# Loading part of q in two transfers: 120 tokens and 8 tokens

## The chip, the cores and the metric

The kernel runs on one core of a Trainium2 chip. A core has five engines that run side by side and wait for each other by semaphores: TensorE (PE, matmuls; its weight loads are shown as PEld), VectorE (DVE), ScalarE (ACT), GpSimd (POOL) and SyncE (SP), which here does nothing but issue transfers. Transfers run on 16 DMA engines. The metric is the device time of one execution in microseconds, the median of several runs.

## The reference

A gated linear attention with a complex gate per channel, then a gated feed-forward block with a residual:

```python
# batch 4, heads 8, tokens 768, head dimension 48
mag = np.sqrt(a_re * a_re + a_im * a_im)
scale = np.minimum(mag, 0.999) / (mag + 1e-06)
a_re_n, a_im_n = (a_re * scale, a_im * scale)
for t in range(S):
    new_re = ar * S_re - ai * S_im
    new_im = ar * S_im + ai * S_re
    S_re, S_im = (new_re + kv, new_im)          # kv: outer product of k[t] and v[t]
    y[:, :, t] = np.einsum('bhd,bhde->bhe', q[:, :, t], S_re)
# x: y as 3072 tokens x 384
g = x @ w_gate;  val = x @ w_val                # 384 -> 1536
ffn_out = gelu(g) * val @ w_out                 # 1536 -> 384
out = x + sigmoid(x @ w_res) * ffn_out
```

All inputs and the output are float32 in HBM. q, k, v and the two gate arrays have the layout batch, head, token, channel, so that one token of one head is a run of 48 numbers, 192 bytes.

## The kernel before

The 768 tokens of a batch element are cut into 6 chunks of 128. A unit is one chunk or a pair of chunks that are worked on together (`units`, L211 to L215). There are 14 units: the first chunk of batch elements 0 and 1 alone, that of 2 and 3 as a pair, then for each later chunk the pairs (0, 1) and (2, 3); the last pair is split into two units. The loop at L643 records the steps of each unit `p` in three functions:

- `prepare(p)` loads the unit's chunks of a_re, a_im, q, k and v (`load`, L368 to L377; one transfer of 192 KB per chunk, at L373), forms cumulated sums of the gate's logarithm and angle (PE at L359 with a triangular matrix, ACT for ln, exp, arctan and sin), multiplies q and k with the magnitudes (DVE, L482: `Qe` from q, `Ke` from k), and with cosine and sine (DVE, L487: `fQ`, `fK`). These are transposed to `QT` and `KT`: on PE (L504) in the first units, and from the ninth unit on by DMA transposes that SP issues (L496).
- `attend(p)` does the chunk's attention: scores (PE, L535), the mask (DVE, L538), the output `x` (PE, L547 and L549), and the carried state (`U`, `Gb`, `Gf`, L565 to L572).
- `forward(p)` transposes x to `xT` (PE, from the fourth unit on a DMA transpose that SP issues, L583), and does the feed-forward block: gate and value matmuls (PE, L605), gelu (ACT, L610), their product `h` (DVE, L611), the residual gate (PE, L620; ACT, L622), the output matmuls (PE, L631), the sum (L635, L638), and the store of 128 tokens that SP issues (L640).

Steps are recorded with what they read and write. The list `ORDER` (L41 to L104) then gives the order in which all of them are issued; it is written out by hand, and each engine's queue is in this order. So SP's queue holds, in one fixed sequence, all 120 loads, 24 stores and 40 transposes; what stands behind a load is issued after it. The weights (`wg`, `wv`, `wo`, `wr`) are loaded by POOL's queue (L340).

A load writes one of 25 wide tiles (`WD`, pool `wd`), which are used in turn by the loaded arrays and by intermediate results; a load waits until the tile's earlier users are done. A transfer's landing is told by one of eight semaphores that SP's transfers take in turn, and an issue waits for the transfer eight issues earlier to have landed.

Of the kernel before, what the change touches and what calls it, by code (L numbers as in the profile page):

```python
# [125 lines left out]
class Plan:  # L126
# [10 lines left out]
    def add(self, eng, kind, fn, reads=(), writes=(), size=1, act=None):  # L137
        deps = set()
        for v in reads:
            deps.update(v.writers)  # L140
        for v in writes:
            deps.update(v.writers)
            deps.update(v.readers)
        stores = [v.store for v in list(reads) + list(writes) if v.store is not None]
        stores = sorted(set(stores), key=stores.index)
        t = Step(eng, kind, fn, deps, stores, size, act)
        t.index = len(self.steps)
        for v in writes:
            v.writers, v.readers = [t], []
        for v in reads:  # L150
            if t not in v.writers:
                v.readers.append(t)
        for x in stores:
            x.users.append(t)
        self.steps.append(t)
        return t
# [30 lines left out]
def kernel(  # L187
# [13 lines left out]
    nc = tc.nc  # L201
# [159 lines left out]
    def flat(t, n):  # L361
        return t[:, 0:n].rearrange("p c h d -> p (c h d)")

    def prepare(p):
        s, n = st[p], size[p]
        N = n * DM

        def load(name, src):  # L368
            s[name] = Wide(name, FP)
            parts = []  # L370
            for i, (b, c) in enumerate(units[p]):
                def fn(i=i, b=b, c=c):
                    nc.sync.dma_start(out=s[name].tile[:, i], in_=src[b, :, c * 128:(c + 1) * 128, :].rearrange("h t d -> t h d"))  # L373
                v_ = s[name].part()
                add("SP", "load", fn, (), [v_])
                parts.append(v_)
            s[name].writers = [x for v_ in parts for x in v_.writers]  # L377
# [49 lines left out]
        if units[p][0][1] < NC - 1:  # L427
            add("POOL", "mrd", lambda: nc.gpsimd.dma_start(
                out=s["mr"].tile[0:n * H, 0, :], in_=P2("E")[127:128].rearrange("p c (h d) -> p (c h) d", d=D)), [s["E"]], [s["mr"]])
# [6 lines left out]
        if olds:  # L436
            src = sorted({where[(b, c - 1)] for b, c in units[p]})
            if len(src) == n == 2 and src[0][0] == src[1][0]:
                add("POOL", "carry", lambda u=src[0][0]: nc.gpsimd.dma_start(
                    out=F("t")[0:1], in_=st[u]["fr"].tile[127:128].rearrange("p c m -> p (c m)"), accum_op=OP.add), olds, [s["t"]])  # L440
            else:
                tp = [s["t"].part() for _ in range(n)]
                for i in range(n):
                    tp[i].writers, tp[i].readers = list(s["t"].writers), list(s["t"].readers)
                    add("POOL", "carry", lambda i=i, u=src[i]: nc.gpsimd.dma_start(
                        out=F("t")[0:1, i * DM:(i + 1) * DM], in_=st[u[0]]["fr"].tile[127:128, u[1]], accum_op=OP.add), [olds[i]], [tp[i]])
# [9 lines left out]
        for i, (b, c) in enumerate(units[p]):  # L456
            if ST:
                add("PE", "cumT", lambda i=i: sums(cth[i], i, F("th"), F("tl")), [s["th"], s["tl"]], [cth[i]])
            else:
# [5 lines left out]
                out=T("fr")[:, i], in0=T("fr")[:, i].bitcast(INT), scalar=-TWO_PI, in1=cth[i].tile,  # L465
# [10 lines left out]
        for m, (src, bi) in enumerate((("fr", zero), ("fw", half_pi))):  # L476
            act("sin", lambda m=m, src=src, bi=bi: nc.scalar.activation(  # L477
                out=T("CS")[:, 0:n * H, m, :], in_=P2(src).rearrange("p c (h d) -> p (c h) d", d=D),
                func=AF.Sin, bias=bi, scale=1.0 if m == 0 else -1.0), [s[src]], [cs[m]], "T")

        for g, src, mag in (("Q", "q", "E"), ("K", "k", "Ei")):
            add("DVE", "qe", lambda g=g, src=src, mag=mag: nc.vector.tensor_tensor(  # L482
                out=T(g + "e")[:, 0:n * H].rearrange("p x u d -> p (x u d)"), in0=flat(T(src), n),
                in1=P2(mag).rearrange("p c m -> p (c m)"), op=OP.mult), [s[src], s[mag]], [s[g + "e"]], n)
        for g in "QK":
            s[g] = Feat(g)
            add("DVE", "feat", lambda g=g: nc.vector.tensor_tensor(  # L487
                out=s[g].tile[:, 0:n * H, 0:DD].rearrange("p x (u d) -> p x u d", u=2),
                in0=T(g + "e")[:, 0:n * H].to_broadcast([128, n * H, 2, D]), in1=T("CS")[:, 0:n * H], op=OP.mult), [s[g + "e"]] + cs, [s[g]], n)
        s["QT"], s["KT"] = [], []  # L490
        for i in range(n):
            for g in "QK":
                s[g + "T"].append(Buf(g + "T"))
                gT = s[g + "T"][i]
                if p >= PE_T:
                    add("SP", "dT", lambda g=g, i=i, gT=gT: nc.sync.dma_start(  # L496
                        out=gT.tile, in_=s[g].tile[:, i * H:(i + 1) * H].rearrange("p x d -> p (x d)"), transpose=True), [s[g]], [gT])
# [185 lines left out]
```

## Time and profile before

| | |
|---|---|
| median of 3 runs | 261.61 us (261.59 to 262.87) |
| profiled execution | 262.78 us, of which 261.0 us from the first to the last instruction (the span) |
| granted PE clock, mean | 0.978 |
| busy: PE, DVE, ACT, POOL | 226.4 us (87%), 225.4 (86%), 214.1 (82%), 94.5 (36%) |
| SP's DMA queue | 157,696 packets, 35.53 MB, 79.4% of the 16 engines' span |
| POOL's DMA queue | 4,448 packets, 3.90 MB, 9.3% |
| the chain that ended last | PE 71%, DMA 11%, ACT 9%, DVE 3%, POOL 2% |
| one load of q, 192 KB | 4.5 us in the median from issue to landing |

The chain that ended last is found by going back from the last instruction, at each step to what released it or to the instruction before it on its engine. The span falls into a first part up to about 76 us, in which the weights come in and PE is busy 46.1 us of 76, and the rest.

```profile
PE   0230992889999999999999999999999999999993
DVE  2589889999899999999999999999999794965363
ACT  4999999899899999999998999999988684241240
DMA  8999999989999997995989896999757919402111
```

Each digit is the busy share, in tenths, of a fortieth of the span (6.5 us); the last row is the mean share of the 16 DMA engines.

```profile
ar<-in_a_re_dram SPq DMA_DIRECT2D x24, 192.0 KB, 4.6
q<-in_q_dram SPq DMA_DIRECT2D x24, 192.0 KB, 4.5
out_dram<-ot SPq DMA_DIRECT2D x24, 192.0 KB, 2.8
xT<-x SPq DMA_TRANSPOSE x20, 3.2
QT<-fQ SPq DMA_TRANSPOSE x10, 3.4
KT<-fK SPq DMA_TRANSPOSE x10, 3.8
```

These are lines of the list of issues: what is written and read, the queue that issues it, how many, the size of one, and the median time from issue to landing in us. In the timeline of SP's queue the q loads of the fifth unit and later start at 62.05 (two), 83.30, 86.49, 92.64, 100.17, 122.58 (two), 124.88 (two), 140.14 (two), 155.12 (two), 159.42, 173.81 (two) and 179.84 us: 18 of the 24.

### The profile page before, as it was taken

Reading aid. Unit: us, or ns where it says so; the run is one execution under the profiler, and the core shown is the slowest. Engines: PE = TensorE matmul, PEld = TensorE weight load, DVE = VectorE, ACT = ScalarE, POOL = GpSimd, SP = SyncE. Lnnn points to the kernel's source line nnn. Section 1 sums busy time; section 2 is a strip of 40 time slices with the busy share of each in tenths; the row PEclk is TensorE's granted clock in tenths of the full one; section 3 lists DMA queues with packets and bytes.
Section 4 is the critical chain, followed back from the end, with each engine's and each line's share of the span. In section 5 each row is a group of like instructions: output and inputs, shape, how many; then the busy total and the mean of one; then the engine's idle time right before and its main releaser. Section 6 shows DMA issues by size and latency. Waiting matters only on the chain.

```text
span 261.0 us, 6358 instructions
## 1 busy us (share of the span) xinstructions
PE 226.4 (87%) x2426; PEld 181.8 (70%) x2426; DVE 225.4 (86%) x404; ACT 214.1 (82%) x355; POOL 94.5 (36%) x114
## 2 busy tenths in 40 slices
PE   0230992889999999999999999999999999999993
PEld 0120772778978977877878877778778777887881
DVE  2589889999899999999999999999999794965363
ACT  4999999899899999999998999999988684241240
POOL 3013086196605743576625634351420001110110
PEclk9999996599999999999999999999999999999998
DMA  8999999989999997995989896999757919402111
GB/s 141 187 187 186 187 194 192 213 163 213 202 184 172 167 186 163 221 146 124 211 149 190 148 179 149 182 168 236 133 114 160 117 23 136 133 3 63 60 63 60
DMA packets 162174, 39.83 MB, mean 153 GB/s; under 512 B 155617, under 2 KB 162145, under 8 KB 162145
## 3 DMA queue, kind: packets, MB, share of 16 engines
q1 hardware_dynamic: 157696, 35.53, 79.4%
q0 software_dynamic: 4448, 3.90, 9.3%
q8 instruction: 19, 0.31, 0.5%
q14 instruction: 11, 0.08, 0.1%
HBM read 31.26 MB, written 4.72 MB: 138 GB/s over the span
## 4 chain that ended last, share of the span: by engine, by line
PE 71%; DMA 11%; ACT 9%; DVE 3%; POOL 2%; SPq 1%; issue 1%; POOLq 0%; DVEq 0%
PE pb L605 32%; PE pb L631 17%; PE pb L359 6%; PE pb L620 4%; PE pb L504 4%; PE pb L535 3%; DMA wo<-in_moe_w_out_dram 3%; DMA wv<-in_moe_w_val_dram 2%; DMA ai<-in_a_im_dram 2%; ACT L652 2%; DMA t<-fr 2%; DMA ar<-in_a_re_dram 2%; POOL t L397 1%; PE pb L549 1%; PE pb L547 1%; ACT CS L477 1%
## 5 line engine op out<-in xcount | busy, mean ns | idle before, releaser
L610 ACT ACTIVATE h<-pb 128x512 bf16<-128x512 f32 (+1 forms) x84 | 41.2, 547 | 23.2 <-PE pb L631 13.0
L605 PE MATMUL pb<-xT,wv 128*128 128x256 bf16 (+1 forms) x504 | 58.1, 257 | 0.4 <-DMA wv<-in_moe_w_val_dram 0.4
L605 PE MATMUL pb<-xT,wg 128*128 128x256 bf16 (+1 forms) x504 | 57.0, 257 | 0.0
L631 PE MATMUL pb<-wo,h 128*128 128x384 bf16 x288 | 56.5, 326 | 0.0
L611 DVE SCALAR_TENSOR_TENSOR h<-h,pb 128x512 bf16<-128x512 bf16 (+1 forms) x84 | 48.5, 602 | 4.2 <-PE pb L605 2.8
L605 PEld LDWEIGHTS <-wg 128*128 128x128 bf16 x504 | 42.9, 98 | 7.1 <-issue 0.8
L652 ACT ACT_TABLE_LOAD x36 | 46.2, 1283 | 1.3 <-PEq L667 0.7
L605 PEld LDWEIGHTS <-wv 128*128 128x128 bf16 x504 | 41.9, 98 | 7.5 <-issue 1.3
L638 POOL TENSOR_TENSOR ot<-ot,x 128x384 f32<-128x384 f32 x16 | 14.6, 913 | 65.0 <-DVE Gb L567 23.4
L631 PEld LDWEIGHTS <-h 128*128 128x128 bf16 x288 | 26.3, 97 | 13.0 <-issue 0.4
L538 DVE TENSOR_TENSOR am<-pb,mask 128x512 bf16<-128x512 f32 x48 | 31.9, 680 | 2.9 <-PE pb L535 2.8
L397 POOL TENSOR_TENSOR t<-t,ai 128x768 f32<-128x768 f32 (+1 forms) x10 | 16.0, 1601 | 18.1 <-DVE fK L487 9.0
L504 PE MATMUL pb<-ident,fK 128*128 128x128 bf16 x112 | 10.0, 246 | 13.5 <-DVE fK L487 13.5
L359 PE MATMUL pb<-th,ut_one 128*128 128x384 f32 x24 | 11.3, 471 | 11.4 <-POOL th L334 11.1
L452 POOL TENSOR_TENSOR tl<-t,th 128x768 fp32r<-128x768 f32 (+1 forms) x10 | 16.5, 1656 | 10.4 <-DVE ll L408 7.8
L635 DVE SCALAR_TENSOR_TENSOR ot<-sg,pb 128x384 f32<-128x384 f32 x24 | 13.1, 547 | 6.8 <-PE pb L631 5.0
L504 PEld LDWEIGHTS <-fK 128*128 128x128 bf16 x112 | 8.4, 112 | 15.0 <-DVE fK L487 14.3
L535 PE MATMUL pb<-QT,KT 96*128 96x128 bf16 x192 | 17.7, 225 | 0.5 <-DMA QT<-fQ 0.4
L535 PEld LDWEIGHTS <-KT 96*128 96x128 bf16 x192 | 13.8, 101 | 3.9 <-issue 2.2
L622 ACT ACTIVATE sg<-pb 128x384 f32<-128x384 f32 x24 | 11.6, 502 | 5.3 <-PE pb L620 2.8
L620 PE MATMUL pb<-wr,xT 128*128 128x384 bf16 x72 | 15.5, 326 | 0.0
L423 ACT ACTIVATE E<-pb 128x384 f32<-128x384 f32 x24 | 11.5, 500 | 3.2 <-PE pb L359 3.0
(91 smaller groups left out, 472.2 us busy)
## 6 DMA issues: line engine op xcount, KB each, us to landing
ar<-in_a_re_dram SPq DMA_DIRECT2D x24, 192.0 KB, 4.6
ai<-in_a_im_dram SPq DMA_DIRECT2D x24, 192.0 KB, 4.6
k<-in_k_dram SPq DMA_DIRECT2D x24, 192.0 KB, 4.4
q<-in_q_dram SPq DMA_DIRECT2D x24, 192.0 KB, 4.5
vf<-in_v_dram SPq DMA_DIRECT2D x24, 192.0 KB, 4.3
out_dram<-ot SPq DMA_DIRECT2D x24, 192.0 KB, 2.8
wg<-in_moe_w_gate_dram POOLq DMA_DIRECT2D x6, 192.0 KB, 5.6
wv<-in_moe_w_val_dram POOLq DMA_DIRECT2D x6, 192.0 KB, 5.9
```

What stands on the lines that cost most here:

```text
L359: nc.tensor.matmul(out=bank.tile, lhsT=ut_one, rhs=x[:, i * DM:(i + 1) * DM], start=(j == 0), stop=(j == 1))
L397: add(e1, "tai", lambda: on[e1].tensor_tensor(out=F("t"), in0=F("t"), in1=flat(T("ai"), n), op=OP.mult), [s["ai"]], [s["t"]], n)
L452: add(e10, "tl", lambda: on[e10].tensor_tensor(out=F("tl"), in0=F("t"), in1=F("th").bitcast(FP), op=OP.subtract), [s["t"], s["th"]], [s["t ...
L504: nc.tensor.transpose(out=tp.tile[:, h, :], in_=s[g].tile[:, i * H + h], identity=ident)
L535: nc.tensor.matmul(out=ap.tile[:, h, :], lhsT=kT.tile[0:DD, u * H // 2 + h, :], rhs=qT.tile[0:DD, u * H // 2 + h, :], start=True, stop=True)
L538: add("DVE", "am", lambda u=u, am=am, ap=ap: nc.vector.tensor_tensor(out=am.tile[:, u * H // 2:(u + 1) * H // 2, :], in0=ap.tile, in1=mask ...
L605: nc.tensor.matmul(out=o_.tile[:, u, :], lhsT=w_[:, k_, (2 * m + u) * 128:(2 * m + u + 1) * 128], rhs=s["xT"].tile[:, k_, 0:n].rearrange(" ...
L610: add("ACT", "gelu", lambda gp=gp, hv=hv: nc.scalar.activation(out=hv(), in_=gp.tile, func=AF.Gelu), [gp], [hh], n, "G")
L611: add("DVE", "h", lambda vp=vp, hv=hv: nc.vector.scalar_tensor_tensor(out=hv(), in0=hv(), scalar=0.5, in1=vp.tile, op0=OP.mult, op1=OP.mul ...
L620: nc.tensor.matmul(out=rp.tile, lhsT=s["xT"].tile[:, k_, i, :], rhs=wr[:, k_, :], start=(k_ == 0), stop=(k_ == KF - 1))
L631: nc.tensor.matmul(out=op_.tile, lhsT=s["h2"].tile[:, k_, i * 128:(i + 1) * 128], rhs=wo[:, k_, :], start=(k_ == 0), stop=(k_ == NF - 1))
L652: plan.run(ORDER, lambda table: nc.scalar.preload_act_table_set(ACT_SETS[table]), after)
```

## The change

From the fifth unit on (`p >= 4`), a chunk of q is loaded by two transfers, issued one right after the other in the place of one: the first brings tokens 0 to 119 to 120 partitions, the second tokens 120 to 127 to the last 8. The bytes, the tile and the step's place in `ORDER` are the same. The loads of the other four arrays, and those of q in the first four units, remain single transfers.

```diff
             for i, (b, c) in enumerate(units[p]):
                 def fn(i=i, b=b, c=c):
-                    nc.sync.dma_start(out=s[name].tile[:, i], in_=src[b, :, c * 128:(c + 1) * 128, :].rearrange("h t d -> t h d"))
+                    rows = src[b, :, c * 128:(c + 1) * 128, :].rearrange("h t d -> t h d")
+                    for lo, hi in ((0, 120), (120, 128)) if name == "q" and p >= 4 else ((0, 128),):
+                        nc.sync.dma_start(out=s[name].tile[lo:hi, i], in_=rows[lo:hi])
                 v_ = s[name].part()
                 add("SP", "load", fn, (), [v_])
```

The built program has 162 copies in SP's queue for 144, and 7 more instructions on DVE that only wait (118 for 111), since a DVE instruction that reads q waits for each of the transfers' semaphores. The other engines' instructions and their order are the same but for one such waiting instruction more on POOL and one fewer on ACT. All lines behind the change have numbers higher by 2.

## Prediction

> **What bounds the kernel now.** I read the busy time by stretch first, then the chain of waits, then SP's own timeline.
>
> ```profile
> core 0: us, PE busy (x) PEld busy (x) DVE busy (x) ACT busy (x) POOL busy (x), PEclk, DMA share, GB/s
> ...
> 163.00:176.00 13.00, 12.62 (x125) 9.84 (x124) 12.80 (x24) 12.85 (x20) 6.07 (x6) 1.00 1.07 174
> 176.00:196.00 20.00, 20.00 (x206) 15.85 (x204) 19.19 (x34) 18.23 (x31) 5.59 (x8) 1.00 0.82 160
> 196.00:225.00 29.00, 29.00 (x313) 23.32 (x311) 24.18 (x48) 19.32 (x31) 0.90 (x1) 1.00 0.70 121
> ```
>
> PE is recorded without idle from 176 to 225 us (49.00 of 49.00 us), and DVE and ACT are over 90% busy until 196. So PE sets the end: a delay that reaches PE there has nothing behind it in which PE could catch up. The PE times are modelled, so a small recovery can't be excluded.
>
> ```profile
> 169.69 0.61 ACT h L610
> 170.30 1.48 SPq L583
> 171.78 0.04 issue
> 171.83 3.25 DMA QT<-fQ
> 175.08 0.14 issue
> 175.22 0.38 PE pb L535 x4
> ```
>
> This is the chain of waits (start, length, what). Once PE has become the bound, the chain leaves it for long, 5.5 us, only here: for ACT, SP's queue and a transpose that SP issues. If SP comes late at 170 us, PE comes late by as much.
>
> ```profile
> 155.12 2.88 SPq L373 DMA_DIRECT2D q<-in_q_dram  x2
> 158.09 1.21 SPq L583 DMA_TRANSPOSE xT<-x  x1
> 159.42 0.51 SPq L373 DMA_DIRECT2D q<-in_q_dram  x1
> 160.03 0.52 SPq L640 DMA_DIRECT2D out_dram<-ot  x1
> 161.01 0.37 SPq L373 DMA_DIRECT2D k<-in_k_dram  x1
> 161.44 0.56 SPq L640 DMA_DIRECT2D out_dram<-ot  x1
> 163.23 1.25 SPq L496 DMA_TRANSPOSE QT<-fQ  x1
> ...
> 173.81 1.80 SPq L373 DMA_DIRECT2D q<-in_q_dram  x2
> ```
>
> SP's timeline (start, time in the issue, transfer). SP works in order. Between issues it loses 0.04 to 0.19 us, here called 0.1; a longer gap is a wait for compute, in which lateness is made up: 162.00 to 163.23 leaves 1.13 us. From 163.23 until 182.55 there is no such gap.
>
> ```profile
> 178.62 0.96 DVE L482 TENSOR_TENSOR Qe<-q,E 128x768 bf16<-128x768 f32 x1 [0.37 <-DMA q<-in_q_dram]
> ```
>
> DVE, too, waits here for the second q load of the pair at 173.81. Issued at 174.5, it landed 4.0 us later, at 178.5.
>
> **The change part by part.** It removes nothing. The last 18 of 24 q loads become 36 transfers with the same bytes, so SP has 18 more issues, each right behind its q load and ahead of everything later in the queue: loads, stores, and the transposes of x, Q and K that PE waits for. Order and engines are otherwise unchanged.
>
> *Price of one more issue.* No SP transfer of fewer than 128 tokens or rows is in the trace, so I bound it by two rows:
>
> ```profile
> L640 SPq DMA_DIRECT2D out_dram<-ot x24: 332/524/1081, 97.0 to 257.9; - x24
> L373 SPq DMA_DIRECT2D q<-in_q_dram x12: 385/939/1661, 122.6 to 179.8; - x12
> ```
>
> Low end: the shortest store, 0.33 us, plus the gap of 0.1: 0.43. High end: the median q load between 122 and 182 us, 0.94, with rounding and gap 1.05. Below the low end lies a full queue: the median 0.94 against a minimum of 0.39 says that SP often stands in an issue until the transfers ahead drain, and the second piece could fall into that time. Then it costs the 0.1 gap alone. I see no reason for a gain in the issue itself. I take 0.75, the middle of 0.43 and 1.05: the piece has few packets, which speaks for the store; but it stands at the q loads' places, where the queue is often full, and it is an HBM load with the same 192-byte rows.
>
> *A rule of the Trainium skill.* The row first: back-to-back full loads occupy SP for 1.0 us each (four from 4.54 in 4.01 us). The Trainium skill, page "DMA: Bandwidth & Descriptors", section "Why a DMA increments its semaphore by 16 and not by 1", lets a transfer use the largest number of engines up to 16 that divides its slowest dimension: 15 for 120 tokens, 8 for 8. My estimate by that page of the Trainium skill: eight of the engines then carry 9 tokens' rows for 8, 0.13 us more on a load of 1.0 us; with 0.13 as the price of a split, all of it is made up and the time stays that of the hidden case below. The section "Rules for kernel authors" on that page of the Trainium skill speaks against the change: two transfers to disjoint partition halves aren't worth it, since they serialize. No view of this trace shows the engines singly.
>
> *SP's lateness at 0.75 each, added up.* Gaps are taken net of 0.1.
> - 62 to 68 us: two splits, 1.5; the gap before 77.08 (2.45, net 2.35) clears it.
> - 83 to 101: four, 3.0; the gaps before 116.13 and 120.41 (net 1.43 and 1.26) leave 0.31. From 76 to 120 us no engine is recorded waiting for a load, so I let nothing of this reach the compute.
> - 122 to 127: four, 3.31; the gap before 132.94 (net 0.70) leaves 2.61.
> - 140 to 142: two, 4.11; the gap before 144.87 (2.81, net 2.71) leaves 1.40, that before 153.84 (net 0.86) 0.54.
> - 155 to 160: three, 2.79; the gaps before 161.01 and 163.23 (net 0.36 and 1.13) leave 1.30.
>
> So the transposes from 163 to 173 us go out 1.3 late, and PE at 175.22, which waits for the last, starts 1.3 minus the 0.14 between landing and start: 1.2 late. Then the pair at 173.81 adds one split ahead of its second load: 2.05 late. That load's own second piece lands later still; I take 0.3 (between 0.07, a sixteenth of a load's 1.05, and the 0.75 by which it is issued later). DVE's Qe had 0.1 to spare: 2.05 + 0.3 - 0.1 = 2.25 late. PE at 181.20 waits for a bank that DVE's h (180.43, 0.68 long) gives free, 0.1 earlier: 2.1 late. The last split, at 179.84, goes into the gap before 182.55 (net 1.44) and isn't on the path. Sum: +2.1 us.
>
> *Hidden edits.* Qe waits for four landings instead of two: 7 more waiting instructions on DVE at 21 ns (the shortest and median of its row on L482), 0.15 us together, in DVE's sequencer beside the instruction before; without that cover, +0.15. SP waits at each issue for the landing of the transfer eight issues back; landings take 4.3 us in the median, 5.2 at most, between 122 and 182 us, and eight issues last 8 x (0.94 + 0.43) / 2 = 5.5 us even where all are q pieces at the low price. What waits behind such a stall is SP's whole queue. Cost 0; if landings grew by 1 us, some 0.7 per pair.
>
> Profiled span 261.0 + 2.1 = 263.1. That execution took 262.78 us, 1.8 around the span and 1.2 above the median of the three runs, so I put the 2.1 on the median: 261.61 + 2.1 = 263.7.
>
> **The rivals.**
> - *Hidden.* At 0.43 the same walk leaves 0 at 120 us, 1.02 at 133, 0 at 145 and 0 at 163; only DVE's wait at 178.62 grows, by 0.43 + 0.3 - 0.1 = 0.6, PE by 0.5: 262.1. For it: the stores' row and the waits inside the issues. Against it: SP's gaps from 132 on are short.
> - *The queue pays in full.* At 1.05: 1.5 at 120, 5.0 at 133, 4.4 at 145, 3.5 at 154, 5.2 at 163, then + 1.05 + 0.3 - 0.1, less 0.15 on the way to PE: 6.3, so 267.9. It decides from about 0.9 each. For it: the DMA share of 1.07 from 163 to 176 us. Against it: 64 packets (8 tokens x 8 heads) for 1,024.
> - *Weights first: faster.* At 70.11 the chain hangs on a transfer of wo on POOL's queue that takes 7.25 us, while SP's loads of q and ai stand in the same engines; the loads of wg, half its size, land in 5.6 in the median. If the splits at 62 to 68 us hold SP's loads back and wo lands in 5.6, PE starts its saturated stretch 1.65 earlier: 260.0. It decides if SP's ai load (68.59) is 1.5 later and PE finds no other wait. Against it: packets of the held loads come in the same microseconds, and the later stretches cost as above.
>
> **How the numbers follow.** The sum above 45% (prices 0.6 to 0.9, whose walks end at 262.6 and 265.8: its own range), hidden 27%, the full price 17%, weights first 11%. A measurement of this kernel can't tell less than 0.5%, 1.3 us, from no change. Slower by more: 41 of the sum's 45 and all 17 of the full price, 58%. Within: 4 + 27 + 3 = 34%. Faster: 8 of the 11, 8%. The range reaches from the weights' side, 260.8 (half of that case outside), to 267.6, just short of the full price.
>
> **What would show it.** 36 q issues on SP from the fifth unit on, with the small ones at 0.4 to 0.7 us; the gap before 163.23 gone; the transposes after it 1 to 1.5 us later; DVE's wait before the Qe at 178.6 over 2 us, or an idle PE there. I am wrong if the small issues last under 0.35 us or the long ones beside them get shorter by as much, if the gaps stay, or if wo at 70 us lands in under 6 us and PE's first stretch starts earlier.

## The result and the profile after

The kernel with the split loads takes 263.37 us in the median of 20 runs (262.12 to 266.00), the kernel before on the same chip 261.95 us (20 runs): a ratio of 1.0050, 95% interval 1.0028 to 1.0072. Beside other runs of the kernel before (262.25 us) it was measured once more: 263.96 us, 1.0090, 1.0058 to 1.0121. So the change costs 0.3 to 1.2%, and some 1.4 to 1.7 us by the medians. The profiled execution took 263.40 us, its span 261.6.

The busy time by stretch, after (columns as before):

```profile
163.00:176.00 13.00, 12.03 (x120) 9.45 (x119) 12.80 (x24) 12.20 (x19) 6.07 (x6) 1.00 0.98 178
176.00:196.00 20.00, 19.82 (x201) 15.55 (x201) 18.09 (x33) 17.94 (x30) 5.61 (x8) 1.00 0.82 154
196.00:225.00 29.00, 29.00 (x313) 23.34 (x312) 24.21 (x47) 19.33 (x31) 0.90 (x1) 1.00 0.66 119
```

PE has 12.03 us for 12.62 between 163 and 176 us and 19.82 for 20.00 up to 196; behind that its record is as full as before. The chain of waits through that place (start, length, what):

```profile
171.60 1.31 SPq L498
...
172.95 0.57 SPq L375
...
173.57 0.66 SPq L375
...
174.27 0.62 SPq L375
...
174.94 0.33 SPq L375
175.27 0.04 issue
175.31 3.34 DMA q<-in_q_dram
...
178.77 0.96 DVE Qe L484
...
180.25 0.36 PE pb L561 x8
```

Before, it went from the transpose straight to PE; now it goes on in SP's queue through the pair of split q loads, four issues (120, 8, 120 and 8 tokens, at 173.57, 174.27, 174.94 and 175.31 us), and comes to PE by way of DVE's Qe. The two waits there, in the engines' timelines:

```profile
174.95 0.38 PE L537 MATMUL pb<-QT,KT 96*128 96x128 bf16 x4 [0.97 <-DMA QT<-fQ]
178.77 0.96 DVE L484 TENSOR_TENSOR Qe<-q,E 128x768 bf16<-128x768 f32 x1 [1.47 <-DMA q<-in_q_dram]
```

They were 0.38 and 0.37 us. SP's timeline ahead of them:

```profile
154.20 3.95 SPq L375 DMA_DIRECT2D q<-in_q_dram  x4
158.25 1.19 SPq L585 DMA_TRANSPOSE xT<-x  x1
159.53 1.07 SPq L375 DMA_DIRECT2D q<-in_q_dram  x2
...
162.38 1.30 SPq L498 DMA_TRANSPOSE QT<-fQ  x1
163.73 1.32 SPq L498 DMA_TRANSPOSE KT<-fK  x1
165.16 0.71 SPq L375 DMA_DIRECT2D k<-in_k_dram  x1
165.92 2.40 SPq L498 DMA_TRANSPOSE KT<-fK  x1
```

To compare executions, I take the distance between two DVE instructions: the mask `am` at 165.05 us before (L538) and the `fK` at 181.03 (L487, the one behind that Qe), 15.98 us apart. In the split's profile they stand at 164.10 and 181.18, 17.08 apart: 1.10 us were lost between them. Single lines of DVE's timeline, first before, then after; those in the middle are the masks of the scores that wait for QT:

```profile
165.05 0.68 DVE L538 TENSOR_TENSOR am<-pb,mask 128x512 bf16<-128x512 f32 x1
176.97 1.28 DVE L538 TENSOR_TENSOR am<-pb,mask 128x512 bf16<-128x512 f32 x2
181.03 0.95 DVE L487 TENSOR_TENSOR fK<-Ke,CS 128x1536 bf16<-128x1536 bf16 x1
```
```profile
164.10 0.68 DVE L540 TENSOR_TENSOR am<-pb,mask 128x512 bf16<-128x512 f32 x1
176.02 1.29 DVE L540 TENSOR_TENSOR am<-pb,mask 128x512 bf16<-128x512 f32 x2
181.18 0.95 DVE L489 TENSOR_TENSOR fK<-Ke,CS 128x1536 bf16<-128x1536 bf16 x1
```

From 84 to 165 us and from 181 us to the last DVE instruction, the two executions keep their distance within 0.1 us; all fourteen profiles below do so within 0.2 us. The difference of the starts, 0.95 us at 165, was there at 84 us already; it is treated below. So the place is known to a few microseconds, and the experiments are read at the same two instructions.

### The profile page after: what moved, and what is told of

Read it like the earlier page. It is cut to its first block, busy times and chain, and to the rows that moved or that the text cites. A ratio compares the mean times of both kernels' runs of the same rounds, so it can differ in the third digit from the quotient of the medians.

```text
span 261.6 us, 6383 instructions
## 1 busy us (share of the span) xinstructions
PE 224.5 (86%) x2426; PEld 179.7 (69%) x2426; DVE 225.3 (86%) x404; ACT 213.9 (82%) x355; POOL 95.0 (36%) x114
## 4 chain that ended last, share of the span: by engine, by line
PE 71%; DVE 8%; DMA 7%; ACT 6%; SPq 2%; issue 2%; POOL 2%; DVEq 0%; ACTq 0%; POOLq 0%
PE pb L607 33%; PE pb L633 18%; PE pb L359 4%; PE pb L506 4%; PE pb L622 4%; PE pb L537 3%; DMA wv<-in_moe_w_val_dram 2%; DMA ar<-in_a_re_dram 2%; PE pb L551 2%; DMA t<-fr 2%; PE pb L549 2%; POOL t L399 1%; SPq L375 1%; PE pb L561 1%; DMA q<-in_q_dram 1%
## 5 line engine op out<-in xcount | busy, mean ns | idle before, releaser
L537 PEld LDWEIGHTS <-KT 96*128 96x128 bf16 x192 | 13.1, 97 | 5.6 <-issue 2.7
```

The lines of the kernel that those rows point to most:

```text
L537: nc.tensor.matmul(out=ap.tile[:, h, :], lhsT=kT.tile[0:DD, u * H // 2 + h, :], rhs=qT.tile[0:DD, u * H // 2 + h, :], start=True, stop=True)
```

## The experiments

Each has the kernel before run beside it on the same chip. "Lost" is the distance of the two DVE instructions less the 15.98 us of the first profile of the kernel before; "QT" is the issue of the transpose at 163.23, moved by the difference at `am`, so that 163.23 means not late; "block" is the time from that issue to the issue of the pair of q loads at 173.81; "pair" is the time the pair takes on SP. In the two kernels with the k loads later, the block holds two issues fewer. Lost and these columns come from one execution each.

| kernel | ratio, 95% interval | lost, us | QT | block | pair |
|---|---|---|---|---|---|
| before, first profile | | 0 | 163.23 | 10.58 | 1.80 |
| before, second profile | | 0.52 | 163.23 | 11.14 | 1.78 |
| the change | 1.0050 (1.0028 to 1.0072) | 1.10 | 163.33 | 11.19 | 2.19 |
| the change, again | 1.0090 (1.0058 to 1.0121) | 1.14 | 163.23 | 11.31 | 2.38 |
| five late splits only | 1.0031 (1.0006 to 1.0055) | 2.23 | 163.76 | 11.51 | 2.10 |
| thirteen others only | 0.9999 (0.9981 to 1.0017) | -0.01 | 163.23 | 10.67 | 1.50 |
| 64 and 64 tokens | 1.0108 (1.0074 to 1.0142) | 3.61 | 164.58 | 11.52 | 2.68 |
| 120, 4 and 4 tokens | 1.0156 (1.0116 to 1.0196) | 3.73 | 164.55 | 11.62 | 2.98 |
| the pair only | 1.0003 (0.9981 to 1.0025) | 0.80 | 163.23 | 11.05 | 2.62 |
| the three at 155 to 160 us only | 1.0013 (0.9992 to 1.0034) | 1.23 | 163.42 | 11.71 | 1.26 |
| the change, the pair swapped | 1.0019 (0.9995 to 1.0042) | -0.35 | 163.23 | 10.33 | 2.19 |
| no split, two k loads later | 1.0006 (0.9980 to 1.0032) | -0.27 | 163.23 | 9.83 | 1.27 |
| the change, two k loads later | 1.0066 (1.0040 to 1.0092) | 1.20 | 163.38 | 10.18 | 2.00 |
| the three, small pieces on POOL | 1.0036 (1.0017 to 1.0055) | 0.92 | 163.23 | 11.58 | 1.61 |

**Only the five splits between 154 and 176 us.**

```diff
-                    for lo, hi in ((0, 120), (120, 128)) if name == "q" and p >= 4 else ((0, 128),):
+                    for lo, hi in ((0, 120), (120, 128)) if name == "q" and p in (10, 11, 12) else ((0, 128),):
```

> Splits only the five q loads of the units 10, 11 and 12, the ones issued between 154 and 176 us; the other thirteen are one transfer again. Theory (the loss is made at one place: five more issues on SP push the xT and QT transposes of 168 to 173 us and the second q load of unit 10 back, and DVE's Qe at 178.6 waits for that load): the whole loss stays, 1.0 to 1.6 us over the kernel before, and the wait of that Qe for its load is 1.0 us or more (0.37 before, 1.47 with all splits). Rival (every split costs its share wherever it stands): 5/18 of 1.4 us, about 0.4 us. Rival (the first stretch up to 76 us moves the time): no difference from the kernel before apart from its spread.

**Only the other thirteen.**

```diff
+                    for lo, hi in ((0, 120), (120, 128)) if name == "q" and p in (4, 5, 6, 7, 8, 9, 13) else ((0, 128),):
```

> Splits the thirteen q loads of the units 4 to 9 and 13 and leaves those of the units 10, 11 and 12 whole. Theory (only the five at 154 to 176 us are paid for; the rest goes into idle time of SP before 116, 120, 133, 145 and 154 us): 0 to 0.4 us over the kernel before, with the wait of unit 10's Qe below 0.9 us. Rival (every split costs its share): 13/18 of 1.4 us, about 1.0 us.

The thirteen cost nothing that can be measured: ratio 0.9999, and DVE's timeline keeps its distance (15.97 us) and its short wait:

```profile
163.59 0.68 DVE L540 TENSOR_TENSOR am<-pb,mask 128x512 bf16<-128x512 f32 x1
...
177.15 0.96 DVE L484 TENSOR_TENSOR Qe<-q,E 128x768 bf16<-128x768 f32 x1 [0.36 <-DMA q<-in_q_dram]
179.56 0.95 DVE L489 TENSOR_TENSOR fK<-Ke,CS 128x1536 bf16<-128x1536 bf16 x1
```

The five alone make the kernel slower, 263.44 against 262.37 us, and their profile loses 2.23 us between the two instructions, half of it at a KT transpose that PE waits 0.99 us for at 169 us. That every split pays alike falls: thirteen of eighteen would have cost some 1.0 us. The interval of the five (0.2 to 1.4 us) doesn't exclude that a part of the change's loss is elsewhere, but no profile shows one.

**Two halves of 64 tokens.** The tuple becomes `((0, 64), (64, 128))`.

> The same eighteen loads in two transfers of 64 tokens each: the same number of issues, but each half on 16 engines instead of 15 and 8. Theory (SP's issues are what is paid): 1.0 to 1.8 us over the kernel before, as with 120 and 8, or a little more since the second issue is then no short one. Rival (the uneven spread over the engines makes the load land late): 0 to 0.7 us, with unit 10's second q load landing within 3 us of its last issue (3.34 with 120 and 8).

**Three transfers.** The tuple becomes `((0, 120), (120, 124), (124, 128))`.

> The same loads in three transfers of 120, 4 and 4 tokens: 36 more issues on SP in place of 18. Theory (issues on SP, with no idle time of SP left before 162 us): the loss more than doubles, 2.5 to 4 us over the kernel before, since the idle time that took the first split's issues is used up; the wait of unit 10's Qe is 2.5 us or more. Rival (the last short piece is what is paid, once for each load, whatever the number of issues): 1.4 to 1.8 us. Rival (it is no more than what the split does to the first stretch): about 1.4 us.

The halves lose more than expected, the three pieces a little more: 265.41 and 266.64 against 262.37 us. What a q transfer takes on SP between 122 and 182 us, large and small pieces together, from the view of the tile q (shortest/median/longest in ns); the change, the halves, the three pieces:

```profile
L375 SPq DMA_DIRECT2D q<-in_q_dram x23: 325/457/1823, 121.9 to 179.8; - x23
```
```profile
L375 SPq DMA_DIRECT2D q<-in_q_dram x22: 595/633/1882, 121.4 to 177.8; - x22
```
```profile
L375 SPq DMA_DIRECT2D q<-in_q_dram x33: 297/442/2253, 122.7 to 178.8; - x33
```

Half the tokens don't halve the issue: behind a transpose 64 take 0.60 us at the least, a whole load 0.51. The trace gives the size of each issue, and the shortest in the first view, 0.33 us, is not one of 8 tokens but of the 120 tokens that come right behind 8; the 8 tokens of the change take 0.43 to 1.16 us from 80 us on. In the last view the 0.30 us are the second piece of 4 tokens; the first, behind 120, takes 0.43 or more. Two halves put more on SP than 120 and 8, and spreading the load evenly over the engines doesn't help. In both kernels QT is 1.3 us late, for the first time visibly, since the idle time of SP ahead of it is used up. What that does is in the chain of waits of the three pieces:

```profile
165.67 0.09 SPq L498
165.75 0.05 issue
165.81 5.57 DMA KT<-fK
171.38 0.05 issue
171.42 0.40 PE pb L537 x4
```

PE then waits 2.7 us for KT (2.6 with the halves), more than KT's issue was late. The Qe doesn't wait for its load in either kernel, against the expectation for the three pieces: the loss has moved to KT.

**Parts of the five.** Only the pair (`p in (10, 11) and i == 1`), and only the three before it (`p in (10, 11) and i == 0 or p == 12`).

> Splits only the two loads issued in a row at 173.8 us (the second q load of the units 11 and 10), two issues more than before. Theory (lateness of SP adds up over the splits at 155 to 160 us and at 173.8 us and is paid once, by the Qe of unit 10): the pair takes about 0.4 us more (2.19 against 1.80 us), the Qe of unit 10 comes 0.3 to 0.6 us later against the work at 165 us, and PE's wait for QT just before 175 us stays at about 0.4 us; the time is 0 to 0.6 us over the kernel before. Rival (the short second piece itself lands late, at about 3.3 us, whatever stands ahead of it): the Qe comes 1.0 us later or more, as with all splits.

> Splits only the three loads issued between 155 and 160 us (q of unit 12, the first q loads of the units 11 and 10), none of them used before 178 us. Theory (they hold up SP, and the KT and xT transposes behind them are issued late): the QT transpose at 171.6 is 0.4 to 1.2 us late against the work at 165 us, PE's wait for it is 0.7 us or more (0.38 before), and the Qe of unit 10 is 0.4 to 1.2 us late; 0.4 to 1.2 us over the kernel before. Rival (the 1.69 us of idle time of SP before 161.0 and 163.2 us take all of it): no shift between 165 and 181 us, the time of the kernel before.

Neither alone gives a time apart from the kernel before (262.21 and 262.43 against 262.07 us). The profiles lose 0.80 and 1.23 us; both are more than the parts they should be, and the second profile of the kernel before, below, says why they can't be taken at face value. The columns tell the parts better. The pair takes 2.00 to 2.62 us on SP where it is split, 1.26 to 1.80 where it isn't: in the mean of six each 2.25 against 1.54, 0.35 us a split. The three loads at 155 to 160 us lengthen SP's stretch there (from the first of them to the end of the last, the xT transpose among them) from 4.52 to 6.50 us against the kernel with only the pair split, and yet QT goes out 0.19 us late: the idle time, 0.46 and 1.23 us in the kernel before, took the rest. In the mean of the profiles the stretch is 4.41 us where the three are whole (five profiles, 3.47 to 4.81) and 6.09 where SP issues them split (six, 5.26 to 6.50): 0.56 us a split. And the block behind QT, in which nothing is split, is 11.71 us long. In this profile the Qe waits 0.87 us, but for a result of ACT (Ei, L426) and not for its load.

**The pair swapped.** In `ORDER`, `1211, 1101` becomes `1101, 1211`: unit 10's second q load, which the Qe waits for, goes ahead of unit 11's.

> All eighteen loads split, but the two loads at 173.8 us change places: the one that the Qe at 178.6 waits for goes first. Theory (that Qe's wait makes the larger part of the loss, PE's wait for QT the rest): the Qe's wait falls from 1.47 us to 0.4 us or less, PE's wait for QT just before 175 us stays near 1.0 us, the work after 181 us is 0.5 to 0.8 us late against that at 165 us (1.11 with the split alone), and the time is about 0.5 us below that of the split alone. Rival (PE's wait for QT is the whole loss, and the Qe has slack behind it): the work after 181 us stays 1.1 us late, the time that of the split alone.

The Qe no longer waits (started 13.12 us behind `am`, against 14.67 in the change), and the time is 262.55 against 262.07 us; the interval, up to 1.0042, lies mostly below the change's first and wholly below its second. But the block was short in this execution (10.33 us) and PE waited only 0.24 us for QT, so this profile doesn't divide the loss between the two waits as was hoped. The others do. In the six profiles in which the pair of masks stands 11.92 us behind `am`, as in the lines above, and the Qe then waits for its load, what is lost is the growth of that wait over the 0.37 us of the first profile, to 0.01 us: 1.10 us in the change, 1.14 the second time, 0.80 with only the pair, 0.52 in the second profile of the kernel before, none with the thirteen. PE's wait for QT, up to 1.05 us in them, isn't felt on DVE.

**SP relieved ahead of the pair.** In `ORDER`, the steps 1309 and 1212 (two k loads, not used before 188 us) move from 166.0 and 173.2 us to behind `1211, 1101, 635`; once without the split, once with it.

> No split. Two k loads that nothing uses before 188 us (second half of unit 12's k at 166.0 us, unit 11's first k at 173.2 us) are issued behind the store that follows the pair of q loads, so that the transposes of 166 to 173 us and the pair come earlier. Theory (SP's issue time ahead of QT and of unit 10's q is what PE and DVE wait for, 0.38 and 0.37 us before): both waits are gone, the work after 181 us is 0.3 to 0.5 us earlier against that at 165 us, and the time falls by 0.3 to 0.5 us. Rival (PE is bound there anyway, the waits have slack): no shift, and the time of the kernel before. Rival (the two loads, now at 176 us, hold up the transposes at 182 us or the vf loads): slower by up to 0.6 us.

> All eighteen splits, and the two k loads of which nothing is used before 188 us issued behind the pair of q loads and the store, as in the kernel without splits above. Theory (SP's time ahead of unit 10's second q load is what is paid; the two k issues held 0.53 and 0.58 us of it): the shift between 165 and 181 us falls from 1.11 us to between -0.3 and 0.4 us, and the time is 0.6 to 1.4 us below the split alone. Rival (the small pieces' transfers, not SP's time, make the loads land late): the shift stays at 0.8 us or more.

Without the split both waits are gone and 0.27 us is gained in the profile, but the time is that of the kernel before (1.0006, 0.9980 to 1.0032). With the split, SP's time alone falls as the explanation: the kernel stays slower (1.0066, 1.0040 to 1.0092). The pair was issued in time (end 175.59, 175.60 in the kernel before, with `am` 0.02 apart), and still 1.20 us was lost, at KT: issued at 164.76, 0.22 us late against `am`, it landed 5.65 us later, and PE waited 1.67. The DMA view between 164 and 172 us shows what lay in between (40 slices of 0.2 us: busy tenths of the 16 engines, and what they moved). First the kernel before, then this one:

```profile
DMA  6589999977999999479999999500010000999999
GB/s 217 192 201 228 223 216 211 181 143 147 202 209 212 207 172 154 73 112 179 225 229 242 266 208 171 10 0 0 0 8 9 11 12 18 259 292 268 288 250 261
```
```profile
DMA  9999999999999999979899900300009999100036
GB/s 224 303 369 368 279 238 224 140 186 268 223 209 245 166 220 193 182 148 215 168 183 109 58 12 9 14 8 10 9 12 260 292 272 273 26 0 0 10 80 113
```

From 169.0 to 170.8 us, here from 168.6 to 170.0, next to nothing moves, in the middle of SP's transposes. Every one of the fourteen profiles has such a stop (under 30 GB/s) between 167.6 and 171.1 us, the longest of each 0.75 to 1.8 us. It isn't peculiar to this place: in the first profile of the kernel before, the rate also stays under 30 GB/s for 1.2 to 1.6 us from 122.2, 144.6 and 156.2 us. In the kernel before, KT has landed when it begins (PE used it at 168.61 without waiting); here it hadn't.

**The small pieces issued by POOL.**

```diff
-                    for lo, hi in ((0, 120), (120, 128)) if name == "q" and p >= 4 else ((0, 128),):
-                        nc.sync.dma_start(out=s[name].tile[lo:hi, i], in_=rows[lo:hi])
+                    for lo, hi in ((0, 120), (120, 128)) if name == "q" and (p in (10, 11) and i == 0 or p == 12) else ((0, 128),):
+                        (nc.gpsimd if lo else nc.sync).dma_start(out=s[name].tile[lo:hi, i], in_=rows[lo:hi])
```

> Splits only the three q loads of 155 to 160 us, as above, but the three transfers of 8 tokens are issued by POOL. The transfers are the same, SP has no issue more than before. Theory (SP's issue time): the KT transpose and the xT transposes at 165 to 170 us come when they came before, and the shift between 165 and 181 us, 1.24 us with all six issues on SP, is 0.4 us or less. Rival (three small transfers more, and 15 engines in place of 16 for the large ones, fill the DMA engines, and the long KT issue of 2.55 us is that): the shift stays at 0.8 us or more.

SP's timeline of this kernel:

```profile
160.62 0.56 SPq L642 DMA_DIRECT2D out_dram<-ot  x1
162.18 1.26 SPq L498 DMA_TRANSPOSE QT<-fQ  x1
163.48 1.32 SPq L498 DMA_TRANSPOSE KT<-fK  x1
164.92 0.61 SPq L375 DMA_DIRECT2D k<-in_k_dram  x1
165.57 2.08 SPq L498 DMA_TRANSPOSE KT<-fK  x1
167.76 2.04 SPq L585 DMA_TRANSPOSE xT<-x  x1
```

The expectation failed. SP was back in time (1.00 us idle before QT; 1.23 in the kernel before), but the second KT and the xT take 2.08 and 2.04 us, and 0.92 us is lost; the time is 262.85 against 262.25. So SP's extra issues aren't needed for the long transposes. POOL issues three transfers more in this kernel, which may cost something by themselves; that wasn't tried apart. So the rival, that the small transfers themselves are paid and not SP's time, isn't excluded by this kernel. As with the three on SP, the Qe waits for ACT's Ei here (0.80 us).

**The change, and the kernel before, once more.** No edit.

> The change as it stands (all eighteen splits of 120 and 8 tokens), a second time, on the chip and beside the runs of the two kernels below. Theory: 1.0 to 1.7 us over the kernel before, and in its profile, as in the first, no shift between 84 and 165 us and 0.8 to 1.6 us between 165 and 181 us. Rival (the first profile's wait of Qe was that execution's own): no shift there, or one as large elsewhere.

> The kernel before once more, for one profile: nothing is changed. Theory (the first 76 us differ from execution to execution, the 0.95 us by which the split's profile is early there is not its doing): this profile's work at 84 us starts 0.3 us or more away from the 84.08 us of the first profile of this kernel, as that of the kernels without an early split did (1.1 to 1.7 us earlier), and there is no shift between 84 and 181 us. Rival (the split load at 62 us lets the weights land earlier): within 0.2 us of the first profile at 84 us.

The change repeats itself: 1.14 us lost, the Qe's wait 1.51 us. The kernel before doesn't: its second profile loses 0.52 us against its first, with nothing split, where one xT transpose takes 2.29 us on SP (1.19 in the first), and

```profile
178.52 0.96 DVE L482 TENSOR_TENSOR Qe<-q,E 128x768 bf16<-128x768 f32 x1 [0.89 <-DMA q<-in_q_dram]
```

So "no shift between 84 and 181 us" was wrong, and half a microsecond between two profiles at this place is no effect of an edit. The start of the full stretch differs from execution to execution, too: the DVE copy at 83.78 us in the first profile (the second to QT, L334, in the row of 83.18 us) is at 83.16 in the second, at 82.05 to 83.28 in the five other kernels that leave unit 4's loads whole, and at 82.30 to 83.78 in the seven that split them.

## Why the prediction was right or wrong

- **The place was right.** All that is lost in the change's two profiles is lost between 165 and 181 us. Both waits named are there, PE for QT at 175 (0.97 us) and DVE's Qe for the second q load (1.47), but only the growth of the second, 1.10 us, is the loss; that PE's lateness at QT counts for itself isn't borne out. The thirteen splits elsewhere are free, as the walk had it for those up to 120 us, and also from 122 to 142, where it carried lateness on.
- **The price of a split was mis-sized, by a gain that the prediction saw no reason for.** 0.75 us was taken between 0.43 and 1.05. The small piece itself isn't far from that: in the pair the first adds 0.67 us with its gap, and the 85 that SP issues in the profiles from 80 us on take 0.52 in the median, up to 1.36, and only four of them under 0.43. But what SP issues right behind a small piece is short. The second load's 120 tokens take 0.33 us (174.94) where the whole load took 1.10 (174.50, the second of the pair at 173.81); a load of another array takes 0.39 us in the median behind a small piece (25 issues) and 1.08 behind a whole q load (35). So one of the prediction's own signs of being wrong was there: the long issues beside the small ones got shorter. Net, a split costs 0.35 us in the pair and 0.56 at 155 to 160 us. The prediction's thought that the piece could fall into time in which SP stands anyway fits this, but no run shows why the next issue is short.
- **So the carried lateness was mis-sized.** The walk left 1.30 us at 163.23; QT went out 0.10 late in one profile and in time in the other. That is the walk of the hidden rival. SP's gap before 144.87 stayed at 1.72 us (2.81 before), the one before 163.23 went to 0.09, as foreseen, and to 0.64 the second time. The halves and the three pieces show the same walk beyond its edge: 1.3 us late, 2.6 and 2.7 us of waiting.
- **What took its place wasn't in the sum.** Against `am`, the second q load (its first piece) was issued 1.39 us later: 0.10 from QT's issue, 0.61 because the block behind it grew from 10.58 to 11.19 us, 0.68 from the pair. The block was counted as unchanged. It holds one transpose of 2.40 us for 1.37. In part that is not the change's: the kernel before had 11.14 us the second time.
- **The tail of 0.3 us was not there.** From the second load's first issue to its landing it was 4.0 us and is 3.71, the small piece included (174.94 to 178.65). 1.39 less 0.29 gives the 1.10 lost; 2.25 was forecast for the Qe.
- **The sum** of 2.1 us is over the 1.4 to 1.7 of the medians and the 1.1 of the profiles (0.6 against the second profile of the kernel before). That the forecast time comes close is in part luck: the walk was too dear by 1.2 to 1.3 us and the tail by 0.6, and a block that was taken for rigid gave 0.6 to 0.7 back.
- **The rivals.** Hidden was right in its walk; its end (+0.5) lies below the measured loss. The full price is out. Weights first: the wait for wo at 70 us is gone from the chain in the change's two profiles, but so it is in one kernel that leaves unit 4's loads whole (the small pieces on POOL), and with unit 4's loads split the stretch after it starts no earlier (83.05 us against 82.89 in the mean of seven profiles each, at the instruction of 83.78).
- **The engines.** The queue has 126 packets more, 18 times 7; the halves add 288, 18 times 16. By the Trainium skill, "DMA: Bandwidth & Descriptors", section "Why a DMA increments its semaphore by 16 and not by 1", each engine used ends with a count of its own: 15 and 8 for 16 would give these 7, and 16 and 16 for 16 these 16. So that part of it agrees. The uneven spread is not what is paid for: with even halves the loss is larger.

**Open.** Why the transposes of 165 to 170 us sometimes hold SP for 2 us and more, and whether the splits make that likelier: the block is 10.58 to 11.14 us in the four profiles with the loads at 155 to 160 whole, 10.33 to 11.71 in the five with 120 and 8 tokens there and the k loads in place, 11.58 with the small pieces on POOL. The stop of the DMA engines is in all of them, so the split doesn't make it; what does isn't known. A late KT, or a backlog that KT stands behind, runs into it, and then costs more than it was late. The loss of the five is shown; its division between SP's issues, the small transfers themselves, the long transposes and the stop is only read from single profiles. The medians lose 1.4 to 1.7 us, more than the 0.6 to 1.1 of the profiles, and where the rest is isn't known.

No kernel beat the one before: moving the two k loads removes both waits without a measurable gain.

## What to carry to other kernels

In this kernel, a DMA issue added to a queue was paid only where the queue had no idle time left ahead of a transfer that a busy engine waited for: find that transfer, and count back to the last gap that clears the queue. Cutting a load in two doesn't halve its issue (0.60 us for half, 0.51 for the whole, each behind a transpose), and what a small piece costs is to be read with the issue behind it. And repeat the profile of the kernel before, before reading half a microsecond out of one.

## What was not expected of the hardware

- The issue time on SP goes less by a transfer's size than by what was issued just before it: 120 tokens take 0.33 us behind 8 tokens (22 of 27 issues) and 0.51 or more behind a transpose; 4 tokens take 0.43 or more behind 120 and 0.30 in the median behind 4.
- The DMA engines nearly stop for 0.75 to 1.8 us between 167.6 and 171.1 us in each of fourteen profiles, whatever SP issues there, and at other places of the program too.
- Two executions of one program keep their distance within 0.1 us from 84 to 165 us, and then differ by 0.52 us over the next 16.
